# Two loads of 768 bytes a partition made one of 1536 in the segment loop of a gated two-branch mixer

## The chip, the cores and the metric

The kernel runs on one core of a Trainium2 chip. The metric is the time of one execution on the device in microseconds (us); lower is better. Times of several runs are given by their median.

## The reference, cut to what matters

Two branches work on the same input x (2048 tokens, 640 wide) and are mixed by a gate. Branch A is recurrent: the tokens are taken in 64 segments of 32; each segment is put behind 8 memory tokens, goes through full attention with 32 heads of 192, and the first 8 output rows become the memory of the next segment. Branch B is a sliding attention with 32 heads of 20.

```python
mem = mem0                                    # 8 rows
for s in range(n_seg):                        # 64 segments
    xs = x[:, s * seg_len:(s + 1) * seg_len, :]     # 32 rows
    h = concatenate([mem, xs], axis=1)              # 40 rows
    q = einsum('btd,dhe->bhte', h, Wq)              # the same for k and v
    scores = einsum('bhqe,bhke->bhqk', q, k) * Dh ** (-0.5)
    scores = where(mask, scores, -1e9)              # idx[:,None] < 8, or causal
    o = einsum('bhqk,bhke->bhqe', softmax(scores), v)
    o = einsum('bhte,hed->btd', o, Wo)
    mem = o[:, :8, :]
    outs.append(o[:, 8:, :])
a = concatenate(outs, axis=1)
g = sigmoid((x * gate_w).sum(-1))
result = g * a + (1 - g) * b                  # b: branch B
```

A segment needs the memory that the one before it made, so the 64 segments run one after the other.

## The kernel before

The program has four stages. `part_b` computes branch B and writes it, already times 1-g, to `bsc_dram`. `prepass` computes what does not depend on the memory: for the last 8 of the 32 tokens of every segment (called z here) it computes keys, queries and values with big matmuls and writes them to `zpk_dram`, whose record for a segment is 128 partitions by 1152 elements: values in 0:384, keys in 384:768, queries in 768:1152 (bf16, so 768 bytes a partition each). `part_a` is the loop over segments, and `part_z` at the end makes the output rows of the last tokens from what the loop stored in `oz_dram`.

In `part_a` the 8 memory tokens and the first 24 tokens of the segment (32 columns, tile `hT`) go through the projections: 8 pieces of queries and keys (`m_qk`, L540, copied out by ScalarE at L545, transposed at L554), the values (`m_v`, L623), the scores (`s_a`, L577, for keys made in the loop; `s_b`, L586, for the z keys), the exponentials (`e_exp`, L594), their normalization (`e_norm`), the product with the values (`pv_half`, L643 and L647), and the output projection (`o_group`, L680), whose result ScalarE copies into `whi` in two halves (L746 and L754). Three and two matmuls with `sel_m` (L690) turn the first 8 rows of `whi` into the memory columns of the next `hT`.

The weights don't fit whole in the on-chip memory: 15 slices of 384 KB a segment are streamed by the queue of SyncE (`wst`, L383 and L381) into 5 buffers; a slice is sent for when a buffer has been used by TensorE.

The order of TensorE and of ScalarE is the order of the source (`tc.manual_schedule`); ScalarE's queue also issues all transfers of the loop other than the weights, in its place among ScalarE's own instructions. A segment's own are: the store of its attention output for the last tokens (L739), the z keys (L513) and z queries (L514) of the next segment, then during the next segment the store of the output before (L772), the z values (L519), branch B's rows (L724) and the next input columns (L509).

One tile `ZQ` of 2144 columns holds several things by column range: exponentials of the first half `Es[0]` in 0:224, z values `Vz` in 224:608, z keys `KTz` in 608:992, the queries `QTa` in 992:2144. Of the queries, 992:1376 is filled by the load of z queries and the rest by the copies of L557. Two ranges are used twice: the exponentials of the second half, `Es[1]`, lie in 608:832, so over part of the z keys, and `whi` lies in 1376:2016. A tile `KZ` of its own takes the z keys as loaded; a GpSimd copy (L515) reorders them into `KTz`.

The calls around the change, at the end of a segment:

```python
                nc.scalar.copy(whi[:, 0:384], pso["oa"][:, 0:384])        # L746
                if s + 1 < nseg:
                    load_z(s + 1)                                         # L513, L514, L515
                    pm = psS.tile([128, 2, 512], F32, tag="S", name="ps_mem")
                for i2 in range(3, 12):
                    o_group("ob", i2)
                    ...
                nc.scalar.copy(whi[:, 384:640], pso["ob"][:, 0:256])      # L754
```

The z queries are first read by `s_a(0)` (L577) of the next segment, the z keys by `s_b(0)` (L586) after that.

Of the kernel before, what the change touches and what calls it, by code (L numbers as in the profile page):

```python
# [10 lines left out]
BF = mybir.dt.bfloat16  # L11
# [13 lines left out]
class _K:  # L25
# [452 lines left out]
    def part_a(self):  # L478
        nc, tc, KC, S = self.nc, self.tc, self.KC, self.S
# [3 lines left out]
        with ctx:  # L483
            pers = ctx.enter_context(tc.tile_pool(name="a_pers", bufs=1))
            work = ctx.enter_context(tc.tile_pool(name="a_work", bufs=1))
            ZQ = pers.tile([128, 224 + 768 + 1152], BF, name="ZQ")
            self.build_sel(pers, ZQ[:, 0:160])
            KTz = ZQ[:, 608:992].rearrange("p (c r) -> p c r", r=32)
            Vz = ZQ[:, 224:608]
            QTa = ZQ[:, 992:2144].rearrange("p (b r c i) -> p b r c i", b=6, r=2, i=8)  # L490
            Es = [ZQ[:, 608 * h:608 * h + 224].rearrange("p (a f) -> p a f", a=2) for h in range(2)]
# [5 lines left out]
            V = [KV[:, f0:f0 + 384] for f0 in (0, 768, 384, 1152)]  # L497
            oTxs = [v.rearrange("p (c q) -> p c q", q=32) for v in V]
            a4 = pers.tile([128, 160], BF, name="a4")
            KZ = pers.tile([128, 384], BF, name="KZ")  # L500

            psm = ctx.enter_context(tc.tile_pool(name="psm", bufs=2, space=bass.MemoryType.PSUM))
            psx = ctx.enter_context(tc.tile_pool(name="psx", bufs=2, space=bass.MemoryType.PSUM))
# [6 lines left out]
                return hT  # L510

            def load_z(s):
                nc.scalar.dma_start(KZ[:], self.zpk_dram[s, :, 384:768])  # L513
                nc.scalar.dma_start(ZQ[:, 992:1376], self.zpk_dram[s, :, 768:1152])  # L514
                nc.gpsimd.tensor_copy(KTz.rearrange("p c (R i) -> p c R i", i=8),  # L515
                                      KZ[:].rearrange("p (R c i) -> p c R i", c=12, i=8))

            def load_vz(s):
                nc.scalar.dma_start(Vz, self.zpk_dram[s, :, 0:384])  # L519
# [2 lines left out]
            for kc in range(KC):  # L522
                nc.scalar.dma_start(hT[:, kc, 0:8], self.mem0[:, kc * 128:(kc + 1) * 128].rearrange("m p -> p m"))
            load_z(0)
            load_vz(0)
            sel_b = tail = store = None

            sched = ctx.enter_context(tc.manual_schedule(engines={mybir.EngineType.PE, mybir.EngineType.Activation}))
            for s in range(nseg):
# [217 lines left out]
                if s + 1 < nseg:  # L747
                    load_z(s + 1)
                    pm = psS.tile([128, 2, 512], F32, tag="S", name="ps_mem")
# [137 lines left out]
```

## Time and profile before

| | |
|---|---|
| median of 3 runs | 1902.32 us (1899.49 to 1911.51) |
| the profiled execution | 1907.39 us, span 1905.7 us |
| TensorE busy | 1729.0 us (91% of the span) |
| ScalarE / VectorE / GpSimd busy | 743.4 / 655.9 / 69.5 us |
| loop, from L746 of the first segment to L746 of the last | 432.27 to 1817.06 us: 1384.79 us for 63 segments, 21.98 each |
| transfers in the loop | DMA engines 90% busy, 291 GB/s |

The span is what the profiler saw from the first to the last instruction; the execution's own time is 1.7 us longer. The profiled execution lies inside the range of the runs, 5.1 us above their median. Busy time of TensorE is that of overlapping matmuls; a line such as `L513` is the line of the kernel's source above.

### The profile page before, as it was taken

Reading aid. Unit: us, or ns where it says so; the run is one execution under the profiler, and the core shown is the slowest. Engines: PE = TensorE matmul, PEld = TensorE weight load, DVE = VectorE, ACT = ScalarE, POOL = GpSimd, SP = SyncE. Lnnn points to the kernel's source line nnn. Section 1 sums busy time; section 2 is a strip of 40 time slices with the busy share of each in tenths; the row PEclk is TensorE's granted clock in tenths of the full one; section 3 lists DMA queues with packets and bytes.
Section 4 is the critical chain, followed back from the end, with each engine's and each line's share of the span. In section 5 each row is a group of like instructions: output and inputs, shape, how many; then the busy total and the mean of one; then the engine's idle time right before and its main releaser. Section 6 shows DMA issues by size and latency. Waiting matters only on the chain.

```text
span 1905.7 us, 91340 instructions
## 1 busy us (share of the span) xinstructions
PE 1729.0 (91%) x41120; PEld 1022.0 (54%) x41135; DVE 655.9 (34%) x2047; ACT 743.4 (39%) x1865; POOL 69.5 (4%) x135
## 2 busy tenths in 40 slices
PE   6998999779999999999999899989999999999989
PEld 3554544335555555555555555555555555555557
DVE  4565433223333333333333333333333333333330
ACT  3776522123333343333333333333443333333340
POOL 4010000010000000000000000000000000000000
PEclk9999999989999999999999999999999999999999
DMA  6510395979889899899989888989999898998991
GB/s 176 177 44 16 100 308 137 303 203 291 282 287 297 283 296 292 287 301 292 303 291 296 284 278 290 295 281 287 297 299 293 289 293 284 295 289 282 294 295 31
DMA packets 299434, 486.88 MB, mean 255 GB/s; under 512 B 99236, under 2 KB 168356, under 8 KB 299044
## 3 DMA queue, kind: packets, MB, share of 16 engines
q1 hardware_dynamic: 182680, 420.92, 67.7%
q10 hardware_dynamic: 116364, 60.12, 11.3%
q8 instruction: 322, 5.28, 1.1%
q14 instruction: 68, 0.56, 0.1%
HBM read 446.61 MB, written 35.91 MB: 253 GB/s over the span
## 4 chain that ended last, share of the span: by engine, by line
PE 73%; DMA 9%; ACT 7%; issue 5%; DVE 3%; ACTq 2%; SPq 0%; DVEq 0%
PE ps_qk L540 22%; PE ps_v L623 12%; PE ps_wo L680 10%; PE ps_qkT L554 6%; PE ps_pre L425 5%; DMA ZQ<-zpk_dram 4%; PE ps_S L577 3%; PE ps_bqk L220 3%; PE ps_z L819 3%; PE ps_oT L643 3%; ACT bP L243 2%; DMA zpk_dram<-ZV 2%; DMA wst<-in_A_Wk_dram 2%; ACT KV L545 1%; DVE KV L653 1%
## 5 line engine op out<-in xcount | busy, mean ns | idle before, releaser
L545 ACT CAST KV<-ps_qk 128x384 bf16<-128x384 f32 x512 | 239.4, 480 | 415.0 <-PE ps_qk L540 411.4
L540 PEld LDWEIGHTS <-hT 128*32 128x32 bf16 x10240 | 237.6, 96 | 192.2 <-issue 75.1
L540 PE MATMUL ps_qk<-wlate_k,hT 128*32 128x384 bf16 x4352 | 248.4, 328 | 11.0 <-ACT ZQ L754 6.6
L623 PE MATMUL ps_v<-wlate_v,hT 128*32 128x384 bf16 x4096 | 228.0, 329 | 6.0 <-issue 5.8
L680 PEld LDWEIGHTS <-KV 128*32 128x32 bf16 x6144 | 172.4, 98 | 111.0 <-DVE KV L653 33.6
L540 PE MATMUL ps_qk<-wres_q,hT 128*32 128x384 bf16 x2560 | 164.8, 331 | 28.5 <-ACT KV L545 15.9
L557 DVE COPY ZQ<-ps_qkT 128x384 bf16<-128x384 bf16 x256 | 91.2, 356 | 250.6 <-PE ps_qkT L554 250.2
L680 PE MATMUL ps_wo<-wlate_oa,KV 128*32 128x384 bf16 x2304 | 160.3, 339 | 12.8 <-issue 4.0
L540 PE MATMUL ps_qk<-wst,hT 128*32 128x384 bf16 x1792 | 154.5, 331 | 1.7 <-issue 1.5
L623 PEld LDWEIGHTS <-hT 128*32 128x32 bf16 x5120 | 113.8, 96 | 70.7 <-issue 12.9
L554 PE MATMUL ps_qkT<-ident,KV 128*128 128x128 bf16 x1536 | 141.2, 221 | 3.8 <-DVE ZQ L616 1.7
L653 DVE CAST KV<-ps_oT 128x192 bf16<-128x192 f32 x256 | 79.9, 353 | 186.4 <-ACT KV L653 186.4
L680 PE MATMUL ps_wo<-wlate_ob,KV 128*32 128x256 bf16 x2688 | 134.9, 280 | 10.2 <-issue 10.2
L554 PEld LDWEIGHTS <-KV 128*128 128x128 bf16 x1536 | 87.6, 97 | 95.0 <-issue 93.7
L680 PE MATMUL ps_wo<-wst,KV 128*32 128x384 bf16 (+1 forms) x1152 | 124.1, 319 | 5.4 <-issue 3.5
L653 ACT CAST KV<-ps_oT 128x192 bf16<-128x192 f32 x256 | 69.8, 325 | 123.7 <-PE ps_oT L647 122.2
L540 PE MATMUL ps_qk<-wlate_q,hT 128*32 128x384 bf16 x1536 | 108.3, 330 | 0.0
L577 PE MATMUL ps_S<-ZQ,KV 128*32 128x40 bf16 (+1 forms) x4096 | 99.6, 186 | 8.3 <-DMA ZQ<-zpk_dram 6.8
L577 PEld LDWEIGHTS <-KV 128*32 128x32 bf16 (+1 forms) x4096 | 77.7, 92 | 47.4 <-issue 10.8
L693 DVE CAST hT<-ps_mem 128x24 bf16<-128x24 f32 x126 | 22.6, 179 | 214.6 <-PE ps_mem L690 214.6
L627 ACT CAST KV<-ps_v 128x384 bf16<-128x384 f32 x128 | 61.4, 479 | 84.1 <-DMA a<-bsc_dram 50.7
L623 PE MATMUL ps_v<-wst,hT 128*32 128x384 bf16 x1024 | 89.1, 336 | 1.2 <-issue 1.2
(130 smaller groups left out, 2214.4 us busy)
## 6 DMA issues: line engine op xcount, KB each, us to landing
wst<-in_A_Wq_dram SPq DMA_DIRECT2D x260, 384.0 KB
wst<-in_A_Wv_dram SPq DMA_DIRECT2D x260, 384.0 KB
wst<-wscr SPq DMA_DIRECT2D x256, 384.0 KB
wst<-in_A_Wk_dram SPq DMA_DIRECT2D x195, 384.0 KB
zpk_dram<-ZS ACTq DMA_DIRECT2D x4, 3072.0 KB
ZQ<-zpk_dram ACTq DMA_DIRECT2D x128, 96.0 KB
wlate_k<-in_A_Wk_dram SPq DMA_DIRECT2D x17, 384.0 KB
wlate_v<-in_A_Wv_dram SPq DMA_DIRECT2D x16, 384.0 KB
```

The source lines that it names most:

```text
L220: nc.tensor.matmul(ps[:, 0:nn], lhsT=wqk[n][:, kc, 4 * g:4 * g + 4, :].rearrange("p h d -> p (h d)"), rhs=xT[:, kc, o0:o0 + nn], start=(kc ...
L425: nc.tensor.matmul(ps[:], lhsT=sls[kc][:, c0:c0 + 128], rhs=zT[:, kc, :], start=(kc == 0), stop=(kc == KC - 1))
L540: nc.tensor.matmul(pq[32 * j:32 * j + 32, 0:384], lhsT=hT[:, kc, :], rhs=sl[:, 384 * j:384 * j + 384], start=(kc == 0), stop=(kc == KC - 1 ...
L545: nc.scalar.copy(st, pq[:, 0:384])
L554: nc.tensor.transpose(pT[:, t, :, :, :].rearrange("p j b i -> p (j b i)"), st[:, 128 * t:128 * t + 128], self.ident[:])
L557: nc.vector.tensor_copy(q_blocks(R)[:, 1:5, :, :].rearrange("p b c i -> p c b i"), pT.rearrange("p t j b i -> p (t j) b i"))
L577: nc.tensor.matmul(pSs[h][32 * j:32 * j + 32, par, 40 * r:40 * r + 40], lhsT=KT[k0:k1, 12 * r + c, :], rhs=q_blocks(R)[k0:k1, :, c, :], st ...
L623: nc.tensor.matmul(pv[32 * j:32 * j + 32, 0:384], lhsT=hT[:, kc, :], rhs=sl[:, 384 * j:384 * j + 384], start=(kc == 0), stop=(kc == KC - 1 ...
L627: nc.scalar.copy(V[R], pv[:, 0:384])
L643: nc.tensor.matmul(out[:, r, t, :], lhsT=V[2 * h + r][ks, f0:f1], rhs=E[ks, par, 40 * r:40 * r + 40], start=(r == 0 and t == 0), stop=Fals ...
L653: cp(oTxs[2 * h + j // 2][:, 6 * (j % 2):6 * (j % 2) + 6, :], pos[j // 2][:, j % 2, 0:240].rearrange("p (c q) -> p c q", q=40)[:, :, 8:40])
L680: nc.tensor.matmul(pso[part][32 * jj:32 * jj + 32, 0:n], lhsT=oTxs[2 * (R // 2) + j // 2][:, 6 * (j % 2) + 3 * (R % 2) + t, :], rhs=o_weig ...
```

## The change

`load_z` loads keys and queries of a segment in one transfer: columns 384:1152 of the record, 1536 bytes a partition, go into `ZQ[:, 608:1376]`, so that the queries land where they did, and the keys as loaded land in 608:992, where the reordered keys were. The reordered keys get a tile of their own, `KTz`, of the size that `KZ` had; the GpSimd copy now reads `ZQ` and writes `KTz`.

```diff
-            KTz = ZQ[:, 608:992].rearrange("p (c r) -> p c r", r=32)
...
-            KZ = pers.tile([128, 384], BF, name="KZ")
+            KTz = pers.tile([128, 12, 32], BF, name="KTz")
...
             def load_z(s):
-                nc.scalar.dma_start(KZ[:], self.zpk_dram[s, :, 384:768])
-                nc.scalar.dma_start(ZQ[:, 992:1376], self.zpk_dram[s, :, 768:1152])
-                nc.gpsimd.tensor_copy(KTz.rearrange("p c (R i) -> p c R i", i=8),
-                                      KZ[:].rearrange("p (R c i) -> p c R i", c=12, i=8))
+                nc.scalar.dma_start(ZQ[:, 608:1376], self.zpk_dram[s, :, 384:1152])
+                nc.gpsimd.tensor_copy(KTz[:].rearrange("p c (R i) -> p c R i", i=8),
+                                      ZQ[:, 608:992].rearrange("p (R c i) -> p c R i", c=12, i=8))
```

## The prediction

> **What bounds the kernel now.** I read the page first, then the waits, the two issuing lines, and two stretches of the timeline.
>
> ```profile
> PE 1729.0 (91%) x41120; PEld 1022.0 (54%) x41135; DVE 655.9 (34%) x2047; ACT 743.4 (39%) x1865; POOL 69.5 (4%) x135
> PE 73%; DMA 9%; ACT 7%; issue 5%; DVE 3%; ACTq 2%; SPq 0%; DVEq 0%
> ```
>
> TensorE is the bound, but its loop is a serial chain, so short waits of TensorE count in full. The chain has 9% of DMA and 2% of ScalarE's queue in it: candidates for this change. The waits say what they really cost:
>
> ```profile
> PE ps_oT L643 <- issue: 20.6, 19, 2.2
> PE ps_wo L680 <- issue: 17.6, 23, 1.3
> PE ps_S L577 <- DMA ZQ<-zpk_dram: 6.8, 10, 1.6
> PE ps_qk L540 <- ACT ZQ L754: 6.6, 17, 1.3
> SPq L383 <- PE ps_qk L540: 410.1, 375, 4.5
> ```
>
> (us in total, times, longest.) TensorE waits ten times for the z queries, 6.8 us in all, not the 4% of the span that the chain gives to that transfer; and 6.6 us for ScalarE's copy L754. The last line shows SyncE's queue waiting for TensorE to free weight buffers: the weight stream is ahead, and 90% busy DMA engines do not yet set the pace. The lines with "issue" are TensorE out of instructions: in the packets of the trace, an instruction fetch (16 KB on queue 8, about 0.96 us) ends 1.2 to 1.6 us before nearly each of these restarts.
>
> Now the issuing lines (ns: least, median, most), and the end of one segment:
>
> ```profile
> L513 ACTq DMA_DIRECT2D KZ<-zpk_dram x64: 326/327/2008, 405.5 to 1817.1; - x64
> L514 ACTq DMA_DIRECT2D ZQ<-zpk_dram x64: 331/398/1468, 406.0 to 1817.5; - x64
> ```
>
> ```profile
> 746.63 0.48 ACT L746 CAST ZQ<-ps_wo 128x384 bf16<-128x384 f32 x1 [1.69 <-PE ps_wo L680]
> 746.63 0.33 ACTq L513 DMA_DIRECT2D KZ<-zpk_dram  x1
> 747.05 1.28 ACTq L514 DMA_DIRECT2D ZQ<-zpk_dram  x1
> ...
> 748.38 0.37 ACT L754 CAST ZQ<-ps_wo 128x256 bf16<-128x256 f32 x1 [1.27 <-PE ps_qk L540]
> 748.80 0.35 PE L540 MATMUL ps_qk<-wlate_k,hT 128*32 128x384 bf16 x4 [0.46 <-ACT ZQ L754]
> ```
>
> L514 holds ScalarE's queue for 1.28 us instead of 0.39, L754 starts 0.05 us after it ends (TensorE, named in brackets, had long been done), and TensorE waits for L754. In the trace these long issues end about 0.38 us after an instruction fetch ends. In another segment the issues are short, and the landing is late:
>
> ```profile
> 790.61 0.33 ACTq L513 DMA_DIRECT2D KZ<-zpk_dram  x1
> 791.03 0.40 ACTq L514 DMA_DIRECT2D ZQ<-zpk_dram  x1
> ...
> 797.10 0.51 POOL L515 COPY ZQ<-KZ 128x384 bf16<-128x384 bf16 x1 [22.52 <-DMA KZ<-zpk_dram]
> 798.20 0.37 PE L577 MATMUL ps_S<-ZQ,KV 128*32 128x40 bf16 x16 [1.64 <-DMA ZQ<-zpk_dram]
> ```
>
> **The change part by part.** I measured every step of the 63 segment changes from the start of L746. Undisturbed, L754 starts at 1.27 us and `s_a(0)` (L577) at 5.78 us.
>
> Term A, one issue less on ScalarE's queue. In 21 of the 63 changes L754 starts right behind the end of L514, 0.17 to 1.29 us late, 8.6 us in all, and `s_a(0)` is late by the same amounts (segment 15: L754 at 1.75 instead of 1.27, `s_a(0)` at 6.26 instead of 5.78). The remaining issue stands where L513 stands, 0.01 us after L746. L513 alone would have held L754 up only where it took more than 1.23 us: once to matter, 2.01 us at 1124.6, leaving 0.8 us. So A is worth 7.9 us where `s_a(0)` doesn't wait for the landing anyway.
>
> What hides the other 42 removed issues is TensorE, which delivers the second output half only at 1.25 us; there the 0.4 us are worth nothing. If an issue of double rows took 0.66 instead of 0.33 us, it would still end before 1.23.
>
> A rule stands against this term. The Trainium skill, "DMA: Bandwidth & Descriptors", section "Issuing engines are not separate DMA queues", holds that the sequencer's time to start a DMA is usually small beside the DMA itself; by it A would be nothing and the sum term B alone. The rows say 0.33 to 1.47 us with a copy queued behind.
>
> Term B, the landing. The page gives no landings for these issues; I took for each the last update of its semaphore before that semaphore's next issue. From the start of L746 the keys land at 4.25 us (median), the queries at 5.60. TensorE resumes 0.04 us after a landing. One transfer issued at 0.01 us lands between these: not before the keys, which are half of it. By another row, transfers of 128 partitions on this queue take 4.47 us with 320 bytes a partition (L509) and 4.71 with 768 (L519), so 0.24 us for 448 bytes, and 0.41 more for another 768: 5.12. The middle of 4.25 and 5.60 is 4.92. I take 5.0, which is 0.6 us earlier than the queries now.
>
> Moving every landing of the queries by x, with the measured time at which TensorE would have been ready, gives for A and B together: x = -1.35 (as the keys): -17.5 us; -0.7: -14.5; -0.43 (only the earlier issue): -12.3; 0: -6.2; +0.3: +1.4; +0.5: +8.0; +1.0: +27.5. At x = -0.6: **-13.7 us**. (B alone at -0.6 is some 6.5.)
>
> Term C, packets. Two packets of 768 bytes take 2 x 36 ns; one of 1536, between 55 ns at 1280 bytes and 121 at 3072, about 64: 8 ns saved, times 8 packets an engine, times 63: 4 us of each DMA engine. Hidden, because the weights are ahead (SyncE's wait above); without that cover, at most 4 us gained. I count zero.
>
> The Trainium skill's same page, section "Specifications", puts the least transfer for full rate at 512 bytes, which both sizes exceed; by it the longer row brings nothing and only the issue counts, x = -0.43 and -12.3 us.
>
> Term D, moved dependences. The keys' GpSimd copy now starts after the whole transfer: at about 5.1 instead of 4.4 us, and ends 0.51 us later. `s_b(0)` reads it at 8.3 us or later; the smallest distance today from the copy's end to `s_b(0)` is 2.4 us. Zero, as long as the landing slips by less than that. The transfer now writes over `Es[1]`, so its issue must wait for `pv_half(1)`; that feeds `o_group`, which L746 itself waits for, so it is done. Behind the issue on ScalarE's queue stands L754, and TensorE behind that; this is the place where a new wait would cost. `e_exp(1)`, the next to write `Es[1]`, comes some 8 us after the copy's end. In the order of issues each semaphore is used again after eight transfers; for L513 the one before is a weight slice issued about 7.3 us earlier (landing after 4.4 us in the median, 7.4 at most), and the removed issue does not change which one it is. Zero.
>
> Sum: 1907.4 - 13.7 = 1893.7 for the profiled execution. It lay 5.1 us above the median of the runs, so against the median: 1902.3 - 13.7 = **1888.6 us**, 0.72% less. About 1%, 19 us, is what a measurement of this kernel can tell from no change.
>
> **The rivals.**
>
> More than counted: 1883 or below. Besides A and B in full (-17.5) the waits for instructions would have to shrink; in the loop L643, L680, L647, L540 and L623 wait 20.6 + 17.6 + 9.8 + 7.0 + 7.0 = 62 us for "issue". With a tenth of that, -24 us: 1878. For it: the DMA engines are 90% busy, and 128 packets of the 1536-byte kind replace 256. Against it: most of these waits come in `pv_half` and `o_group`, before L746, when no z load is under way.
>
> Little comes of it: A and B are found, and given back at the next wait, an instruction fetch or L754. -4 to +3 us, about 1902. For it: the fetches are not moved by the change. Against it: they come at fixed places of TensorE's program, so they should come earlier with it.
>
> Slower: the one transfer lands later than the queries do today. The place is `s_a(0)`, the price +8 us at 0.5 us later and +27.5 us at 1.0 later (1930), and it decides from 0.3 us later on, where A is used up. For it: today 17 of 63 segments start `s_a(0)` within 0.1 us of the landing, so there is no reserve. Against it: 320 to 768 bytes cost just 0.24 us, and the issue itself comes 0.42 us earlier.
>
> It doesn't do what it says: rows of 1536 bytes are cut into packets of 768 again. Then x = -0.43 and -12.3 us, hardly another time: 1890. Against it: queue 10 carries packets of 1280 bytes, queue 1 of 3072.
>
> **How the numbers follow.** Forecast (-8 to -18 us, cut packets included) 0.52; more than counted 0.28; little 0.10; slower 0.10. Faster by over 1% is the second and a little of the first's lower end: 0.30. Slower by over 1% needs a landing 0.8 us late or a dependence that I missed: 0.09. Within 1%: 0.61. The range goes from 1876 (-17.5 and a tenth of the instruction waits, less 2 for the runs' own spread) to 1908 (landing 0.4 us late); the forecast's own is 1884 to 1894.
>
> **What would show it.** Right: one issue of 0.33 us at L512, L754 late behind it in at most a few segments; "PE ps_S <- DMA ZQ" below 3 us, "PE ps_qk <- ACT ZQ L754" (two lines up in the new numbering) below 2; landing near 5.0 us after L746; packets of 1536 bytes on queue 10, 8192 of them. Wrong: a landing later than 5.9 us, a long issue in many segments, or the waits for "issue" changed by more than the sum.

## The result, and the profile after

The changed kernel takes 1885.86 us (median of 20 runs, 1876.93 to 1898.02) against 1898.30 us for the kernel before (20 runs, the three of the table ahead of the prediction among them): ratio 0.9944, 95% interval 0.9924 to 0.9964, which is 10.6 us less (6.8 to 14.4). A second comparison on another occasion, 12 runs against 35, gave 0.9975 (0.9951 to 0.9999), 4.7 us less (0.2 to 9.3). So there is a gain, of a quarter to a half of a per cent, though the second interval all but touches nothing.

The profiled execution of the changed kernel took 1898.02 us, the longest of the 20, its span 1896.3 us (before: 1905.7). Lines of the source are two lower than before from `load_z` on. The page first, busy times and the chain that ended last:

```profile
PE 1726.3 (91%) x41120; PEld 1022.6 (54%) x41135; DVE 656.8 (35%) x2047; ACT 743.8 (39%) x1865; POOL 69.5 (4%) x135
PE 78%; ACT 6%; issue 5%; DMA 5%; DVE 4%; ACTq 1%; SPq 0%; DVEq 0%
```

No engine does less work; the chain has lost DMA (9% to 5%) and ScalarE's queue (2% to 1%). The waits of TensorE (us in total, times, longest):

```profile
PE ps_wo L678 <- issue: 19.3, 22, 1.7
PE ps_oT L641 <- issue: 14.8, 15, 1.8
PE ps_qk L538 <- issue: 8.8, 14, 1.3
PE ps_S L575 <- DMA ZQ<-zpk_dram: 1.7, 2, 0.9
PE ps_qk L538 <- ACT ZQ L752: 0.6, 1, 0.6
```

The two waits that the change was priced by fell from 6.8 to 1.7 us and from 6.6 to 0.6 us. The waits for instructions ("issue") did not fall as a whole: over all lines of TensorE they add up to 67.6 us before and 68.2 us now. The one issue that is left:

```profile
L512 ACTq DMA_DIRECT2D ZQ<-zpk_dram x64: 326/327/1868, 403.7 to 1806.6; - x64
```

Its median is 327 ns for twice the bytes: the length of the rows costs the issuing queue nothing. Now a segment change, from the timeline:

```profile
918.58 0.48 ACT L744 CAST ZQ<-ps_wo 128x384 bf16<-128x384 f32 x1 [0.97 <-PE ps_wo L678]
918.59 0.33 ACTq L512 DMA_DIRECT2D ZQ<-zpk_dram  x1
...
919.86 0.37 ACT L752 CAST ZQ<-ps_wo 128x256 bf16<-128x256 f32 x1 [0.79 <-PE ps_wo L678]
920.94 0.35 PE L538 MATMUL ps_qk<-wst,hT 128*32 128x384 bf16 x4 [0.79 <-issue]
...
922.27 0.51 POOL L513 COPY KTz<-ZQ 128x384 bf16<-128x384 bf16 x1 [20.12 <-DMA ZQ<-zpk_dram]
```

The second output copy (L752) now starts 1.28 us after the first, the undisturbed time. But 0.3 us after its start TensorE falls idle for 0.79 us, with no instruction: a fetch of 16 KB had ended 1.04 us after L744 began, 1.3 us before TensorE's restart. Waits of this kind turned out to be where a part of the gain went.

The table takes the 63 segment changes of each profile apart, in us summed over them, from the start of the first output copy: how late the second copy started right behind an issue; when the queries landed (median, each); how long `s_a(0)` waited for that; the waits for instructions from 1.0 to 4.2 us after the copy; and all by which `s_a(0)` came later than 5.78 us. These are my sums over the trace's instructions and semaphore updates. The wait for the landing comes out larger than the profile's own line (9.7 against 6.8 us before), because the profile counts from the modelled end of the last matmul, and my sum from when the next one would have started, some 0.17 us earlier for each of the 17 waits.

```
kernel                     behind issue  landing  wait for it  instr. waits  s_a(0) late  ratio of time
before                       8.7 (21x)    5.60       9.7          9.0          39.8       1
before_again                 5.9 (17x)    5.54       6.2          7.1          30.5       -
own_tile_two_loads           9.5 (21x)    5.61       8.4          6.9          40.1       1.0013
queries_first                7.3 (14x)    4.25       0.2          7.8          27.4       0.9985
tiny_second_issue            8.5 (21x)    4.90       0.1          9.3          30.7       0.9965
two_tiny_issues             30.4 (46x)    4.69       0.8          5.2          48.4       1.0059
one_issue_short_rows         0.3 ( 1x)    5.28       7.9         11.4          32.8       0.9973
changed kernel               0.9 ( 2x)    4.72       3.0          9.8          26.1       0.9944
changed_again                0.0          5.01       1.3         14.7          30.0       0.9975
changed_third                0.2 ( 1x)    5.12       0.4         13.9          33.4       -
load_before_first_copy       0.0          3.31       0.0         10.7          28.8       0.9953
load_behind_second_copy      0.0          6.09      20.2         10.2          42.2       1.0025
queries_then_keys_behind     0.0          4.50       0.0         17.9          34.5       0.9973
```

The sums of instruction waits depend on which waits are put into the stretch. Counting all that begin in it gives 16.1 us for `changed_third` and 19.1 us for `queries_then_keys_behind`, and the table's values elsewhere.

One correction to the table ahead of the prediction: 432.27 to 1817.06 us are 62 steps of the loop, not 63, so 22.34 us each (22.18 in the changed kernel, 1374.92 us from 431.70 to 1806.62).

### The profile page after: what moved, and what is told of

It reads as the page before. It is cut to its first block, busy times and chain, and to the rows that moved or that the text cites. A ratio compares the mean times of both kernels' runs of the same rounds, so it can differ in the third digit from the quotient of the medians.

```text
span 1896.3 us, 91089 instructions
## 1 busy us (share of the span) xinstructions
PE 1726.3 (91%) x41120; PEld 1022.6 (54%) x41135; DVE 656.8 (35%) x2047; ACT 743.8 (39%) x1865; POOL 69.5 (4%) x135
## 2 busy tenths in 40 slices
DMA packets 290217, 486.86 MB, mean 257 GB/s; under 512 B 98212, under 2 KB 159140, under 8 KB 289828
## 3 DMA queue, kind: packets, MB, share of 16 engines
q10 hardware_dynamic: 107148, 60.12, 11.2%
q8 instruction: 322, 5.28, 1.1%
## 4 chain that ended last, share of the span: by engine, by line
PE 78%; ACT 6%; issue 5%; DMA 5%; DVE 4%; ACTq 1%; SPq 0%; DVEq 0%
PE ps_qk L538 24%; PE ps_wo L678 12%; PE ps_v L621 12%; PE ps_qkT L552 6%; PE ps_pre L425 5%; PE ps_S L575 3%; PE ps_oT L641 3%; PE ps_z L817 3%; PE ps_bqk L220 3%; ACT bP L243 2%; DMA zpk_dram<-ZV 2%; ACT KV L543 2%; DVE KV L651 1%; PE ps_bv L207 1%; PE ps_Z L606 1%
## 5 line engine op out<-in xcount | busy, mean ns | idle before, releaser
L621 PEld LDWEIGHTS <-hT 128*32 128x32 bf16 x5120 | 113.8, 96 | 74.0 <-issue 15.4
```

The lines of the kernel that those rows point to most:

```text
L621: nc.tensor.matmul(pv[32 * j:32 * j + 32, 0:384], lhsT=hT[:, kc, :], rhs=sl[:, 384 * j:384 * j + 384], start=(kc == 0), stop=(kc == KC - 1 ...
```

## The experiments

The theory: two waits, the second output copy behind a second issue (A) and the first scores behind the landing of the queries (B). The rivals: fewer packets on busy DMA engines, and dependences that go when the reordered keys no longer share columns with `Es[1]`. The times are ratios to the kernel before on the same chip, with 95% intervals.

**Only the tile moved.** `KTz` has its own tile, the loads are two.

```diff
-                nc.scalar.dma_start(ZQ[:, 608:1376], self.zpk_dram[s, :, 384:1152])
+                nc.scalar.dma_start(ZQ[:, 608:992], self.zpk_dram[s, :, 384:768])
+                nc.scalar.dma_start(ZQ[:, 992:1376], self.zpk_dram[s, :, 768:1152])
```

> Two loads of 768 bytes as before, but with the reordered keys in a tile of their own, as in the changed kernel. Theory (two waits: ScalarE's copy behind the second issue, and scores waiting for the landing of the queries): both waits stay, so the time of before, ratio 1.000 +- 0.002; about 20 of 63 second issues over 0.45 us, queries landing at 5.6 us after the first output copy starts. Rival A (fewer packets on busy DMA engines): also 1.000. Rival B (the gain is from the dependences that go when the keys no longer share their columns with the exponentials): 0.994, as the changed kernel.

1.0013 (0.9989 to 1.0037), and both waits are as before:

```profile
PE ps_qk L539 <- ACT ZQ L753: 7.5, 17, 0.9
PE ps_S L576 <- DMA ZQ<-zpk_dram: 6.4, 8, 1.6
```

The dependences are out. This profile and `before_again` serve below as further profiles of the kernel before.

**Queries first.** The kernel before with the two issues exchanged.

> The kernel before with the two loads in the other order: queries first, then keys. Theory: the landing term alone. Queries land where the keys did, about 4.3 us after the first output copy starts, which takes away the wait of the scores (-9 us by the table of shifts at x = -1.35); the second issue still holds the second output copy up in about 20 segment changes, 8 us. Ratio 0.995. Keys land at 5.6 and their copy ends at 6.1, before 8.3: nothing. Rival A (packets): 1.000, since packets are as before. Rival B: 1.000.

0.9985 (0.9964 to 1.0005). The mechanism is as expected: landing at 4.25 us, the wait for it gone (9.7 to 0.2 us), the copy still held up. The time is not: the interval excludes the 0.995 that I expected and holds the 1.000 that both rivals stated. The wait that is gone from the profile is not found in the time (2.8 us less, from 6.8 less to 0.9 more), and the runs do not say why. Its one profile is better than its runs (span 1884.7 us, runs 1885.47 to 1898.20), so the table's 27.4 us is no fair sample of it.

**A second issue without bytes.** The changed kernel, with

```diff
+                nc.scalar.dma_start(dz[:], self.zpk_dram[s, :, 0:2])
```

> The changed kernel with a second issue behind the one load, of 4 bytes a partition into a tile that nothing reads. Theory: it gives back the issue term and keeps the landing: the second output copy starts late behind an issue in about 20 of 63 segment changes (2 in the changed kernel), the landing stays near 4.7 us, so -8 us against before, ratio 0.996, that is 6 us slower than the changed kernel. Rival A: as the changed kernel, 0.994, as 512 bytes are next to nothing. Rival B: 0.994.

0.9965 (0.9934 to 0.9995), between the two kernels as expected: just clear of the kernel before, but not of the changed kernel, so the time alone does not exclude the rivals' 0.994. The profile is clear; the waits and the added issue:

```profile
PE ps_qk L540 <- ACT ZQ L754: 6.2, 12, 1.1
```

```profile
L514 ACTq DMA_DIRECT2D dz<-zpk_dram x64: 331/392/1972, 406.8 to 1805.7; - x64
```

512 bytes in all, and the copy starts late behind the issue 21 times, 8.5 us, as with the real second load. The lateness of term A comes from the issue, not from its bytes.

**One issue, short rows.** The changed kernel with its load in two pieces of 768 bytes a partition, 16 columns apart.

```diff
-                nc.scalar.dma_start(ZQ[:, 608:1376], self.zpk_dram[s, :, 384:1152])
+                nc.scalar.dma_start(ZQ[:, 592:1392].rearrange("p (g f) -> p g f", g=2)[:, :, 0:384],
+                                    self.zpk_dram[s, :, 384:1152].rearrange("p (g f) -> p g f", g=2))
```

> The changed kernel with its one load written as two pieces of 768 bytes a partition, 16 columns apart, so that one issue makes 256 packets of 768 bytes, as many as before. Theory: the issue term in full, the landing at 5.0 to 5.2 us (the earlier issue), so -12 us, ratio 0.994 to 0.995. Rival A (packets): the time of before, 1.000. Rival B: 0.994.

0.9973 (0.9942 to 1.0005): half the changed kernel's gain in the first comparison, as much as its gain in the second, and too wide to tell my 0.994 to 0.995 from rival A's 1.000. The profile:

```profile
PE ps_S L576 <- DMA ZQ<-zpk_dram: 5.5, 5, 2.3
```

Term A came in full (0.3 us left behind the issue). The landing is at 5.28 us, 0.56 later than with long rows in the first profile of the changed kernel (0.16 to 0.27 later than in its other two), and the scores wait 7.9 us for it. So in the profile the length of the rows is not nothing: the prediction's last rival, rows cut into packets of 768, said "hardly another time", and the wait left over is 5 to 7.5 us more than with long rows. One profile of this kernel is behind that number, and its time does not show it.

**The load behind the second copy.** The changed kernel, `load_z(s + 1)` moved behind L752's copy.

> The changed kernel with its load issued behind the second output copy (L752) instead of before it. Theory (issue and landing): no issue holds the second copy up, but the landing moves 1.3 us later, from 4.7 to 6.0 us after the first output copy starts, 0.4 us later than the queries land in the kernel before; by the table of shifts (A with x = +0.4) +5 us against before, ratio 1.001 to 1.004, and +14 us against the changed kernel. In the profile: no second copy late behind an issue; the scores wait for the landing in more than half of the segments, some 15 to 20 us in all. Rival (fewer packets, whenever they are issued): 0.994 as the changed kernel.

1.0025 (1.0000 to 1.0050), within the expected 1.001 to 1.004. Landing at 6.09 us, 20.2 us of waiting in the sums, 39 starts of `s_a(0)` within 0.1 us of the landing:

```profile
PE ps_S L575 <- DMA ZQ<-zpk_dram: 12.0, 24, 1.5
```

Fewer packets alone are worth nothing here: the same transfer 1.3 us later takes the gain away. The packets rival is out in the form "whenever they are issued". The price of a landing 0.5 us late (the slow rival of the prediction), +8.0 us by the prediction's table of shifts, lies within the measured +4.7 us (0 to 9.5).

**The load ahead of the first copy.** It changes places with the store of the attention output (L739 before).

> The changed kernel with two issues of ScalarE's queue exchanged: the load of the next segment's z keys and queries takes the place of the store of the attention output (L739 of the kernel before), ahead of the first output copy, and that store stands behind the copy. Theory: the landing comes about 0.7 us earlier, near 4.0 us, which takes most of the 3 us of waiting that the changed kernel has left, and changes nothing else: ratio to before 0.992 to 0.994, 0 to 3 us below the changed kernel. Rival (the landing is set by how much lies ahead of it in the queue, and now only the weights do): landing at 3.2 us or earlier, the same time. Other rival: an issue ahead of the first copy that an instruction fetch holds up delays that copy and all behind it: 8 us slower than the changed kernel, 0.998.

0.9953 (0.9922 to 0.9983), the changed kernel's time within the intervals. The landing comes at 3.31 us, earlier than the expected 4.0 and near the first rival's 3.2. The issue's place explains it: the load is issued 1.2 us ahead of the first copy (median) and lands 4.51 us after its issue, against 4.71 in the changed kernel. No wait for it is left; that was worth at most 3 us and doesn't show. A copy delayed by an issue ahead of it does not show either: none of its 63 load issues in the loop took over 0.34 us.

**Queries in the gap, keys behind the second copy.** The kernel before, with its loads taken apart.

```diff
                 nc.scalar.copy(whi[:, 384:640], pso["ob"][:, 0:256])
+                if s + 1 < nseg:
+                    load_zk(s + 1)      # KZ and its GpSimd copy
```

> The kernel before with its two loads taken apart: the queries at the place of the first issue, the keys and their GpSimd copy behind the second output copy. Theory: one issue is left between the two output copies, as in the changed kernel, and the queries land alone at about 4.2 us: issue term -8 us and landing term -9 us, -17 in the sum, less what is given back: ratio 0.991 to 0.994, as good as the changed kernel or better, with 768-byte rows. Keys: issued at 1.3 us, landing near 6, copy done near 6.6, needed at 8.3: nothing. Rival (packets): 1.000, since there are as many as before. Rival (the long row itself brings the gain): 0.997 or more.

0.9973 (0.9947 to 0.9998): with as many packets of 768 bytes as before, a gain of 5.1 us (0.4 to 10.0), a third of the 17 us that the two terms promise and short of the expected 0.991 to 0.994. It is also the time that the rival of the long row stated (0.997 or more), so the time does not settle that rival; the profile speaks against it, since both waits are gone with short rows. Something else has come (timeline):

```profile
1064.70 0.33 ACTq L516 DMA_DIRECT2D KZ<-zpk_dram  x1
...
1067.09 0.34 PE L543 MATMUL ps_qk<-wst,hT 128*32 128x384 bf16 x1 [2.00 <-issue]
```

TensorE waits 2.00 us for instructions just behind the second copy; 17.9 us in this stretch over the loop, against 7 to 9 in the profiles of the kernel before.

**The changed kernel again.** For the spread between profiles.

> The changed kernel once more, for a second profile beside these. Theory: ratio 0.994; second copy late behind an issue in 1 to 4 segment changes, landing at 4.6 to 4.9 us, TensorE waiting 1 to 4 us for it; the waits for instructions within 5 us of the first profile's.

0.9975 (0.9951 to 0.9999); the expected 0.994 lies outside. Issue as expected, landing at 5.01 (expected at most 4.9), 1.3 us of waiting. Its instruction waits in the stretch are 14.7 us.

**Two tiny issues, and one more profile of each kernel.** By now the table showed that kernels with two issues between the copies have fewer instruction waits behind them than kernels with one or none. Two theories: the copy's lateness passes in full to the end, or about half is given back, since the fetch that holds an issue up also leaves TensorE without instructions.

> The changed kernel with two issues of 4 bytes a partition behind its load, so three issues between the output copies. Undisturbed the third ends at 1.16 us, before the second copy is due at 1.27, so only issues held up by instruction fetches delay it: in 25 to 35 of 63 segment changes, 13 to 22 us in all (8.5 with one tiny issue, 0 to 0.9 without). Theory, full pass-through: every microsecond of this reaches the end, so 13 to 20 us above the changed kernel, ratio to before 1.001 to 1.005. Theory, half given back: the fetch that holds the issue up also leaves TensorE without instructions a little later, so a copy that is on time saves only about half; then 6 to 11 us above the changed kernel, ratio 0.998 to 1.000, and TensorE's waits for instructions from 1.0 to 4.2 us after the first output copy below 9 us (8 in four kernels with two issues, 12.5 in six with one or none).

1.0059 (1.0030 to 1.0089). I had the third issue's end wrong: undisturbed it makes the copy 0.07 us late, and all in all the copy is late behind it 46 times, 30.4 us. The waits:

```profile
PE ps_qk L542 <- ACT ZQ L756: 25.2, 29, 2.3
PE ps_qk L542 <- issue: 4.3, 7, 1.3
```

29.5 us more lateness than in the changed kernel; the time is 22 us above it by the first ratio (1.0059 against 0.9944, of 1896), 16 us by the second (against 0.9975). So 0.54 to 0.74 of it reaches the end by the middle values; the intervals of the ratios widen that to 0.3 to 0.97. Neither theory came out whole. The time, 16 to 22 us above, lies about where full pass-through put it (13 to 20 us) and not where the other did (6 to 11), but both had reckoned with 13 to 22 us of lateness and not with 30. The instruction waits in the stretch are the lowest of all, 5.2 us, as the second theory said.

> The kernel before, for a second profile. Both theories: second copy late behind an issue in about 21 segment changes, 8 to 9 us; scores waiting 8 to 10 us for the landing. Half given back: TensorE's waits for instructions from 1.0 to 4.2 us after the first output copy at 6 to 9 us. Full pass-through: no relation, anything from 7 to 18 us.

The landing wait (6.2 us) and the lateness (17 times, 5.9 us) are below what I expected, which shows how far one profile of the same kernel can lie from another. The instruction waits are 7.1 us.

> The changed kernel, for a third profile. Both theories: second copy late behind an issue in 0 to 3 segment changes, landing at 4.6 to 5.1 us, TensorE waiting 1 to 4 us for it. Half given back: waits for instructions from 1.0 to 4.2 us after the first output copy at 10 us or more. Full pass-through: no relation, 7 to 18 us.

Instruction waits 13.9 us; the landing is 0.02 us above the expected range, the wait for it 0.4 us, below it.

In all, the stretch from 1.0 to 4.2 us has 5.2 to 9.3 us of instruction waits in the six profiles with two or three issues between the copies, and 9.8 to 17.9 in the seven with one or none. The border is thin: counted by where a wait ends, the means of the groups are 9.4 and 15.4 us and the groups overlap, with up to 12.4 us in the first and from 11.8 us in the second.

## Why the prediction was right, point by point

**The sum.** Forecast 1888.6 us, -13.7 against its base of 1902.3. Measured -10.6 (6.8 to 14.4) and, in the second comparison, -4.7 (0.2 to 9.3). The direction and the two places are right; the size is too large by 3 us in the first comparison and by 9 in the second, which lies outside the forecast's own 8 to 18 us, next to the rival "little comes of it". That the measured 1885.86 us lies so near the forecast 1888.6 is in part luck: the kernel before came out 4.0 us lower in 20 runs than in the three that were the base.

**Term A, the issue** (7.9 us). The lateness behind the issue went from 8.0 us (mean of three profiles with two loads: 8.7, 5.9, 9.5) to 0.4 (0.9, 0.0, 0.2). Right as a wait; the tiny issue shows that the issue alone makes it. As time, A alone is the difference between the kernel with the tiny issue and the changed kernel, 4.0 us less or 1.9 us more (0.9965 against 0.9944 and 0.9975): not resolved.

**Term B, the landing** (5.0 us; some 6.5 us). Landing at 4.72, 5.01 and 5.12, on the number. The wait for it went from 8.1 us (9.7, 6.2, 8.4) to 1.6 (3.0, 1.3, 0.4): 6.5 us. Right as a wait; as time it is not shown alone, and with the queries loaded first, where the wait went too, the time fell by 2.8 us (from 6.8 less to 0.9 more). The two waits are not independent either: of the three profiles of the changed kernel, those with more instruction waits have less wait for the landing, although the landing itself is later.

**The step that failed** is "`s_a(0)` is late by the same amounts": I passed all of A on to the end. In the trace of before it is so in 12 of the 21 changes, to within 0.01 us, and in the other 9 `s_a(0)` is later by more; but it is not so when A is taken away. My reading: the fetches that hold an issue up fall into the same microsecond in which TensorE stands for the copy; with the copy on time, TensorE runs out of instructions behind the same fetch instead. In the same three profiles of each kernel the instruction waits in this stretch rose from 7.7 to 12.8 us, 5.1 us given back (5.8 or 5.9 with the stretch cut the other ways). -7.7 - 6.5 + 5.1 = -9.1 us, between the two measured values; the table's own last column fell by 7.0 us (36.8 to 29.8), so some 2 us of the account have no place. The prediction had this as a rival ("given back at the next wait, an instruction fetch") and took it as all or nothing; it was a third of the two terms together, and two thirds of A.

The segments tell where it was given back. In 17 of the 63 changes the second copy was late in at least two of the three profiles with two loads. There the lateness fell from 5.7 to 0.4 us a profile, the instruction waits that begin in the stretch rose from 3.2 to 8.5, and `s_a(0)` came no earlier (13.9 us late in all before, 14.1 after), although choosing the segments by their lateness before favours a fall. In the other 46 the instruction waits went from 4.5 to 5.1 us, and `s_a(0)` came earlier by 7.2 us (22.9 to 15.7).

The same account, late copy plus wait for the landing plus instruction waits against the mean of the three profiles, fits seven other kernels within the intervals of their ratios, which are 4 to 6 us either way: +12.6 us for two tiny issues (measured +11.2), +6.6 for the load behind the second copy (+4.7), +1.0 for the own tile (+2.5), -4.2 for short rows (-5.1), -5.9 for one tiny issue (-6.6), -5.9 for the loads taken apart (-5.1), -13.1 for the load ahead of the first copy (-8.9). It doesn't fit the queries first: -8.5 against -2.8 (-6.8 to +0.9). So the shift of the waits is what the profiles show; that the same fetch does it is read from its times beside the waits, and no run took a fetch away.

The Trainium skill, "Runtime: NRT & Kernel Launch", section "Instruction fetch mechanics", holds that the fetch of instruction pages is mostly hidden. Here it is not: TensorE waits 54 to 70 us of the execution for instructions, in every profile. In the kernel before, 47 of the 49 such waits over 0.5 us in the loop's six main lines of matmuls ended 1.2 to 1.6 us after the end of a 16 KB fetch.

**Term C, packets.** One of 1536 bytes took 65 ns in the median (estimate: 64), and 290217 packets are left of 299434. No effect on the weights' pace is seen: the DMA engines are 90% busy in the loop as before and move 293 GB/s instead of 291. Long rows land earlier than the same bytes in short ones (4.72 to 5.12 against 5.28 us), which counts in B.

**Term D, dependences.** Zero, as said: the keys' copy ends at 5.4 us (median) in the changed kernel, with at least 1.9 us to `s_b(0)`, and the moved tile alone changes nothing.

**The rule on the issuing engine's time.** It would have set A to nothing. As a wait A is real and large; as time, by the sum above, some 2.5 us of it are left, a third; no run measured that third clear of noise.

**The rival that doesn't do what it says** fell: there are 8192 packets of 1536 bytes on queue 10.

## What to carry to other kernels

Two transfers of neighbouring rows are worth joining for the issue that goes and for the earlier landing, not for the bytes; look for an instruction that stands in the issuing engine's queue right behind them, and for the first reader. Before a wait is booked as gain, ask what else was waiting at the same time: here, as far as the profiles tell, the same fetch held up the issue and, behind it, TensorE, so that a wait of some 8 us was worth about 2.5. And one profile is not enough for a sum of ten microseconds: three profiles of one kernel gave 26 to 33 us for the same sum.

## What the runs showed of the hardware that I had not expected

A DMA issue on ScalarE's queue takes 0.33 us where it stands first and 0.39 to 0.40 as the second of two, whether the second moves 96 KB or 512 bytes, and 0.33 us for 192 KB in one. The longest took 2.6 us and ended 0.38 us after the end of an instruction fetch; of the 22 issues over 0.7 us in the kernel before, 21 ended 0.15 to 0.39 us after the end of a fetch packet. Long rows (1536 bytes) landed at 4.7 to 5.1 us, as many bytes in 768-byte pieces at 5.3.

Times go with the granted clock: over 197 runs of these kernels it lay between 0.976 and 0.990, and within one kernel 0.001 of it goes with 1.8 us (correlation -0.63). With the clock taken out by this common slope, the changed kernel stands 8.3 and 9.9 us below the kernel before (two sets of runs, standard error 1.4 and 1.1 us). The others have a standard error of about 1.5 us: load ahead of the first copy 10.1 below, short rows 8.0, one tiny issue and the loads taken apart 6.7 each, queries first 4.2, own tile 1.0 above, load behind the second copy 6.1 above, two tiny issues 10.4 above.

By these numbers the two tiny issues stand 18.7 and 20.3 us above the changed kernel, 0.63 and 0.69 of the 29.5 us by which the copy is later, and one tiny issue 1.6 and 3.2 us above it, near the 2.5 us left of A but not clear of nothing. One issue with short rows gains nearly what the changed kernel does, with as many packets as before. That speaks against the packets rival, and it leaves nothing shown in time for the length of the rows. It is also more than the account gives for A without B (-4.2), so how A and B share the gain stays open.
